# Linear attention feeding an expert router: scores for 64x64 diagonal blocks only, a state in the middle of each chunk, masks on GpSimd

## The chip, the cores and the metric

The kernel runs on one core of a Trainium2 chip. The time is the device time of one execution in microseconds (us), median of three runs; lower is better. A profile is one more execution, recorded by the hardware profiler. The core's engines are TensorE (PE: matmuls and transposes; its weight loads are listed as PEld), VectorE (DVE), ScalarE (ACT), GpSimd (POOL) and SyncE (SP, which here issues most DMAs). Each engine works through its own queue in order, and engines wait for each other on semaphores. Matmul results go to PSUM, of which this kernel uses eight banks; its other tiles are in SBUF.

## What is computed

Gated linear attention with a decay for each channel, then a mixture of experts in which each token goes to one expert. All arrays are float32; B, H, S, D = 4, 8, 768, 48; the 8 x 48 = 384 channels of a token are its row for the router; 8 experts, hidden width 1024.

```python
for t in range(S):
    state = alpha[:, :, t, :, None] * state + np.einsum('bhd,bhe->bhde', k[:, :, t], v[:, :, t])
    y[:, :, t] = np.einsum('bhd,bhde->bhe', q[:, :, t], state)
x = y.transpose(0, 2, 1, 3).reshape(B * S, H * D)
logits = normalized(x) @ normalized(expert_emb).T / tau
e = argmax(logits); g = softmax(logits)[e]
out = g * (relu(x @ w1[e]) @ w2[e])
```

## The kernel before, in words

**Chunks and steps.** The 3072 tokens are 24 chunks of 128 (`NS` = 24; six chunks, `NCH`, to a batch row). Channels lie on partitions after a transpose: a pair of heads, each padded from 48 to 64 channels, fills 128 partitions, so a chunk is a tile of 128 x 512 (4 head pairs x 128 tokens). The main loop (L716) runs `s` = 0 to 26, and a step `s` holds stages of several chunks: chunk `s` is decayed, chunk `s-1` gets its scores, chunk `s-2` its output in columns (channels on partitions), chunk `s-3` its output in rows. "Chunk 20's scores" below are thus made in step 21.

**One chunk, stage by stage.** `load` (L450 to L455) fetches alpha in two pieces, k and q of chunk `s` and v of chunk `s-1` through SP's queue, two steps ahead. `decays` transposes alpha (`pa`) and k (`pk`) on TensorE; VectorE scans alpha backwards (`r`, L477) and multiplies k by it (`kr`, L484); q is transposed too (`pq`). `queries` copies q out of PSUM on ScalarE (`qc`, L493). `decay_queries` scans alpha forwards on VectorE (`a`, L506) and multiplies q by it on GpSimd (`qs`, L510). `scores` multiplies `kr` and `qs` for the whole 128 x 128 block of each head, in 16 matmuls of 64 x 64 x 128 columns; the even heads are masked to the causal half by VectorE (L577, times `causal`), the odd heads copied by ScalarE (L578) and masked by GpSimd (`affine_select`, L579). `keys_back` transposes `kr` back (`pkb`; copied by ScalarE to `kb`, L527); `update` multiplies `kb` and v into `pd`, to which VectorE adds the decayed old state (L560); GpSimd decays the state (`dec`, L535). `mix_states` multiplies the old state with the queries, `mix_chunk` v with the scores, into one PSUM bank for the even and one for the odd heads; ScalarE copies both to `ycols` (L621). `rows` turns them into rows and makes the logits in the same matmuls (16 of 64 x 64 x 56 columns); ScalarE copies rows and logits out (L649, L652), VectorE adds the logits (L653).

**Routing.** Every few chunks (`GROUPS`) `choose` picks each token's expert on VectorE and counts tokens into `before` (mostly on GpSimd, L340; for chunks 15 and 23 on VectorE). `place`, two or four steps later, works out each token's row with a few matmuls, and `to_rows` scatters one chunk of 128 tokens (L311, an indirect DMA issued by GpSimd, one or two in a step, queued behind `qs` of the step). After chunk 15 the first expert is chosen (`first_expert`) and `fetch_early` (L181) loads 256 of its tokens; on SP this stands ahead of `weights(0)` (L141, L144), the 3 MB of that expert's weights.

**The tail.** In steps 24 to 26 the last chunks are finished while TensorE does the first layer for the early tokens (`first_layer_early`, `phe`, 8 products), then the last chunks are scattered, and the experts follow, one after another, from about 158 us to the end.

**Order.** PE's order is written out by hand: `in_turn` queues each group of matmuls behind the one before. `issue_after` does so for other engines. Orders left open are settled by the compiler's scheduler. PSUM: three banks rotate for the transposes (`ps_tr`), two hold scores, two `pyx` (also rows of one half and the ranks of `place`), one the state update and the other half of the rows.

Of the kernel before, what the change touches and what calls it, by code (L numbers as in the profile page):

```python
# [9 lines left out]
FP32 = mybir.dt.float32  # L10
# [17 lines left out]
def kernel(  # L28
# [50 lines left out]
    causal = consts.tile([P, 1, P], FP32)  # L79
# [120 lines left out]
    with ExitStack() as c1:  # L200
        keep = c1.enter_context(tc.tile_pool(name="keep", bufs=1))
        work = c1.enter_context(tc.tile_pool(name="work", bufs=2))
        ps_tr = c1.enter_context(tc.tile_pool(name="ps_tr", bufs=3, space=PSUM))
# [15 lines left out]
        inr = keep.tile([P, NP * P], FP32, name="inr")  # L219

        def fixed_parts():
# [14 lines left out]
            make_upper_triangular(nc, causal[:, 0], val=1.0, diag=True)  # L236
# [35 lines left out]
        def prepare_first(a0):  # L272

            p0 = ps_tr.tile([P, NP, NS], FP32, tag="tr", name="p0")
            for p in range(NP):
                tr(
                    p0[:, p], a0[:, 2 * p : 2 * p + 2].rearrange("s h d -> s (h d)"),
                    ident[:NS, :NS],
                )
            nc.vector.tensor_copy(al0, p0)  # L280
# [18 lines left out]
        def turn_logits():  # L299

            pe = ps_tr.tile([P, 2, NP // 2, E], FP32, tag="tr", name="pe")
# [40 lines left out]
        def place(g, total=False):  # L342
# [4 lines left out]
            bank = y_bank(1)[:, 0 : (GMAX + 1) * E].rearrange("p (s e) -> p s e", e=E)  # L347
# [82 lines left out]
        def turned(t, name):  # L430
            pt = ps_tr.tile([P, NP * P], FP32, tag="tr", name=name)
# [32 lines left out]
        def decays(s):  # L464
# [10 lines left out]
            pa = turned(at_s[i], "pa")  # L475
# [5 lines left out]
            pk = turned(kt_s[i], "pk")  # L481
# [3 lines left out]
            d["pq"] = turned(qt_s[i], "pq")  # L485
            d["a"] = pa, r

        def queries(s, copied):

            d = st[s]  # L490
            d["qc"] = qc = work.tile([P, NP * P], FP32, name="qc")
            with tc.issue_after(copied.ins) if copied else ExitStack():
                nc.scalar.copy(qc, d["pq"])  # L493

        def decay_queries(s):
# [13 lines left out]
            d["qs"] = qs = work.tile([P, NP, P], FP32, name="qs", bufs=4)  # L509
            by_pool = nc.gpsimd.tensor_tensor(  # L510
                qs.rearrange("p n t -> p (n t)"), d["qc"], a, ALU.mult
            )
# [3 lines left out]
            d["last"] = by_dve, by_pool  # L516

        def keys_back(s, ps=ps_tr, tag="tr"):

            if s % NCH == NCH - 1 or "kb" in st[s]:  # L520
                return
            kr = st[s]["kr"]
            pkb = ps.tile([P, NP * P], FP32, tag=tag, name="pkb")
# [5 lines left out]
        def decay_state(s):  # L529

            if s % NCH == 0:
                return
            d = st[s]
            dec = d["dec"] = work.tile([P, NP, DP], FP32, name="dec", bufs=3)
            nc.gpsimd.tensor_tensor(  # L535
                dec, carried["state"], d["end"].to_broadcast([P, NP, DP]), ALU.mult
            )

        def update(s):

            c = s % NCH
            if c == NCH - 1:
                return
            d = st[s]
            kb, vt = d["kb"], vt_s[s % NBV]
            pd = ps_mm.tile([P, NP, DP], FP32, tag="mm", name="pd")
            for p in range(NP):
                for hh in range(2):
                    h = 2 * p + hh
                    mm(  # L550
                        pd[DP * hh : DP * hh + DP, p],
                        lhsT=kb[:, h * DP : (h + 1) * DP],
                        rhs=vt[:, h],
                        start=True, stop=True,
                    )
            carried["state"] = state = work.tile([P, NP, DP], FP32, name="state")
            if c == 0:
                nc.vector.tensor_copy(state, pd)
            else:
                nc.vector.tensor_tensor(state, pd, d["dec"], ALU.add)  # L560

        def scores(s):
# [3 lines left out]
            d["sm"] = sm = [work.tile([P, NP, P], FP32, name=f"sm{hh}") for hh in range(2)]  # L566
            sc = [ps_sc.tile([P, NP, P], FP32, name=f"sc{hh}") for hh in range(2)]
            for p in range(NP):
                for i in range(2):
                    to = slice(i * HALF, (i + 1) * HALF)  # L570
                    for hh in range(2):
                        sl = slice(DP * hh, DP * hh + DP)
                        mm(
                            sc[hh][to, p], lhsT=kr[sl, p, to], rhs=qs[sl, p],
                            start=True, stop=True, skip_group_check=True,
                        )
            nc.vector.tensor_tensor(sm[0], sc[0], causal.to_broadcast([P, NP, P]), ALU.mult)  # L577
            nc.scalar.copy(sm[1], sc[1])  # L578
            d["masked"] = nc.gpsimd.affine_select(  # L579
                out=sm[1], in_=sm[1], pattern=[[0, NP], [1, P]], base=0,  # L580
                channel_multiplier=-1, compare_op=ALU.is_ge, fill=0.0,
            )


# [3 lines left out]

        def y_bank(hh):
            return ps_y.tile([P, 512], FP32, name=f"pyx{hh}")  # L590

        def mix_states(s):
            d = st[s]
            d["pyx"] = pyx = [y_bank(hh) for hh in range(2)]
            dec = d.get("dec")
            if dec is not None:
                for q in range(NQ):
                    for j in range(2):
                        for i in range(2):
                            hh, p = i, 2 * q + (i + j) % 2  # L600
                            sl, to = slice(DP * hh, DP * hh + DP), DP * (p % 2)
                            mm(
                                pyx[hh][to : to + DP, q * P : (q + 1) * P],
                                lhsT=dec[sl, p], rhs=d["qs"][sl, p],
                                start=(q == 0), stop=False, skip_group_check=True,
                            )

        def mix_chunk(s):

            d = st[s]  # L610
            pyx, sm, vt = d["pyx"], d["sm"], vt_s[s % NBV]
            d["yT"] = yT = [work.tile([P, NQ, P], FP32, name=f"ycols{hh}") for hh in range(2)]
            for hh in range(2):
                for p in range(NP):
# [770 lines left out]
```

## Time and profile before

| | |
|---|---|
| median of 3 runs | 412.09 us (411.66 to 412.46) |
| the profiled execution | 410.29 us, of which 408.4 us are the span from its first to its last instruction |
| granted TensorE clock, mean | 0.998 |
| PE busy | 394.4 us (97%) |
| DVE busy | 287.2 us (70%) |
| POOL busy | 221.2 us (54%) |
| ACT busy | 195.9 us (48%) |
| attention steps: first and last group of scores | 12.6 and 139.6 us |

The busy times are over both parts of the program, attention (to about 158 us) and experts. A busy PE need not be one at its peak, as matmuls are pipelined. Times inside the profile are counted from the start of the span. In the lists below, `64*64 64x128` after a matmul means that 64 x 64 of the array is used, with 128 columns streamed; a float32 matmul appears as two instructions, a transpose as one.

### The profile page before, as it was taken

How to read it: one execution, taken by the hardware profiler on the slowest of the kernel's cores; microseconds unless marked ns; L12 is line 12 of the kernel's file. 1: busy time of each engine (PE TensorE's matmuls, PEld its weight loads, DVE VectorE, ACT ScalarE, POOL GpSimd, SP SyncE). 2: the span in 40 equal slices, each digit the busy share in tenths (PEclk: the TensorE clock that was granted, in tenths of full speed). 3: DMA queues.
4: the chain of work that ended last, by engine and by line, in shares of the span. 5: the costliest groups of instructions: out<-in, count | busy, mean ns of one | idle time of the engine just before them, and what ended most of it. 6: DMA issues, size and time to landing. Idle time of an engine off the chain costs nothing. (4 is left out here: it accounts for less than half of the span.)

```text
span 408.4 us, 12552 instructions
## 1 busy us (share of the span) xinstructions
PE 394.4 (97%) x4954; PEld 352.6 (86%) x4954; DVE 287.2 (70%) x634; ACT 195.9 (48%) x481; POOL 221.2 (54%) x288
## 2 busy tenths in 40 slices
PE   7999999999979989999999999999999999999994
PEld 6889989889879777779989889899979979979974
DVE  6899989799799517863695695792694388497530
ACT  3455554555535534564743734824551662662320
POOL 7365687777665447712844835812851582581001
PEclk9999999999999999999999999999999999999999
DMA  9999999999998893786405607406502900001001
GB/s 138 160 161 157 157 189 178 186 188 190 203 184 155 313 377 113 208 324 243 162 18 200 220 19 242 171 19 209 206 19 60 351 3 33 27 2 49 8 17 44
DMA packets 119379, 60.28 MB, mean 148 GB/s; under 512 B 102287, under 2 KB 113816, under 8 KB 119312
## 3 DMA queue, kind: packets, MB, share of 16 engines
q1 hardware_dynamic: 115208, 49.14, 50.1%
q0 software_dynamic: 3728, 10.16, 6.9%
q8 instruction: 46, 0.75, 0.8%
q14 instruction: 21, 0.17, 0.1%
q10 hardware_dynamic: 376, 0.05, 0.1%
HBM read 49.69 MB, written 11.45 MB: 150 GB/s over the span
## 5 line engine op out<-in xcount | busy, mean ns | idle before, releaser
L852 POOL DMA_INDIRECT out_dram<-y,sx x25 | 24.5, 981 | 101.2 <-DVE y L1161 42.3
L982 DVE TENSOR_TENSOR hT<-pq,hT 128x512 f32<-128x512 f32 x63 | 43.6, 692 | 46.1 <-PE pq L1082 44.3
L1082 PE MATMUL pq<-xT_m,w_m 128*128 128x128 f32 x560 | 67.2, 276 | 0.0
L1082 PEld LDWEIGHTS pq<-xT_m,w_m 128*128 128x128 f32 x560 | 64.8, 192 | 0.3 <-issue 0.3
L510 POOL TENSOR_TENSOR qs<-qc,a 128x512 f32<-128x512 f32 x24 | 30.6, 1275 | 33.2 <-DVE a L506 24.1
L1034 POOL TENSOR_TENSOR w_m<-w_m,w 128x512 f32<-128x512 f32 x30 | 43.2, 1446 | 1.4
L965 PE MATMUL pyo<-w,hT 128*128 128x384 f32 x128 | 42.6, 487 | 0.0
L1082 PE MATMUL pq<-xT_m,w 128*128 128x128 f32 x280 | 38.4, 277 | 0.6
L987 ACT ACTIVATE hT<-hT 128x512 f32<-128x512 f32 x35 | 22.1, 631 | 31.3 <-DVE hT L982 31.3
L1082 PEld LDWEIGHTS pq<-xT_m,w 128*128 128x128 f32 x280 | 34.9, 192 | 2.1 <-issue 1.8
L965 PEld LDWEIGHTS pyo<-w,hT 128*128 128x128 f32 x128 | 23.8, 191 | 14.8
L477 DVE TENSOR_TENSOR_SCAN r<-pa,inr 128x511 f32<-128x511 f32 x24 | 29.2, 1216 | 6.3 <-PE pa L194 6.1
L311 POOL DMA_INDIRECT xs<-x,dest x24 | 24.2, 1009 | 11.1 <-DVE x L653 6.2
L506 DVE TENSOR_TENSOR_SCAN a<-pa,ini 128x512 f32<-128x512 f32 x24 | 29.3, 1223 | 1.0
L1154 PE MATMUL pq<-w_m,hT_m 128*128 128x192 f32 x168 | 28.4, 326 | 0.0
L191 PE MATMUL sc<-qs,kr 64*64 64x128 f32 x768 | 27.5, 277 | 0.5 <-issue 0.5
L1154 PEld LDWEIGHTS pq<-w_m,hT_m 128*128 128x128 f32 x168 | 27.5, 190 | 0.0
L191 PE MATMUL pyx<-sm,vt 128*64 128x128 f32 x384 | 26.7, 280 | 0.1
L191 PEld LDWEIGHTS pyx<-sm,vt 128*64 128x64 f32 x384 | 20.4, 136 | 4.7 <-issue 3.4
L1034 POOL TENSOR_TENSOR w_m<-w 128x512 f32<-128x512 f32 x12 | 15.3, 1275 | 15.9 <-PE pq L1082 15.9
L191 PEld LDWEIGHTS sc<-qs,kr 64*64 64x64 f32 x768 | 22.3, 137 | 1.2 <-issue 0.9
L649 ACT COPY lg<-pyx 128x32 f32<-128x32 f32 x24 | 4.4, 185 | 38.8 <-PE px L191 38.8
(229 smaller groups left out, 916.5 us busy)
## 6 DMA issues: line engine op xcount, KB each, us to landing
w<-in_moe_w_dram SPq DMA_DIRECT2D x16, 1536.0 KB, 7.9
kt<-in_k_dram SPq DMA_DIRECT2D x24, 192.0 KB, 4.0
qt<-in_q_dram SPq DMA_DIRECT2D x24, 192.0 KB, 4.9
vt<-in_v_dram SPq DMA_DIRECT2D x24, 192.0 KB, 5.3
xg<-xs SPq DMA_DIRECT2D x22, 196.5 KB, 7.8
at<-in_alpha_dram SPq DMA_DIRECT2D x24, 168.0 KB, 4.8
xg<-xs SPq DMA_DIRECT2D x8, 98.2 KB
at<-in_alpha_dram SPq DMA_DIRECT2D x24, 22.5 KB, 4.4
```

The source lines that it names most:

```text
L191: last["pe"] = nc.tensor.matmul(*args, **kwargs)
L311: ins = nc.gpsimd.indirect_dma_start(out=xs, out_offset=bass.IndirectOffsetOnAxis(ap=rows, axis=0), in_=x, in_offset=None, bounds_check=E ...
L477: nc.vector.tensor_tensor_scan(r[:, L - 2 :: -1], pa[:, L - 1 : 0 : -1], inr[:, L - 2 :: -1], 1.0, ALU.mult, ALU.add,)
L506: d["a_scan"] = by_dve = nc.vector.tensor_tensor_scan(a, pa, ini, 0.0, ALU.mult, ALU.add)
L510: by_pool = nc.gpsimd.tensor_tensor(qs.rearrange("p n t -> p (n t)"), d["qc"], a, ALU.mult)
L852: ins = nc.gpsimd.indirect_dma_start(out=out, out_offset=bass.IndirectOffsetOnAxis(ap=col, axis=0), in_=y, in_offset=None, bounds_check=N - 1,
L965: pe[:] = [nc.tensor.matmul(py, lhsT=hT[:, f], rhs=w2_t[:, f], start=(f == 0), stop=(f == FT - 1),)]
L982: dve[:] = [call(*args, **kwargs)]
L987: act[:] = [call(*args, **kwargs)]
L1034: by(to, x, y, op)
L1082: pe[:] = [nc.tensor.matmul(to[:, f], lhsT=left[:, f * P : (f + 1) * P], rhs=right, start=start and f == 0, stop=stop, skip_group_check=Tr ...
L1154: pe[:] = [nc.tensor.matmul(to, lhsT=left[:, f], rhs=right[:, f], start=start and f == 0, stop=stop and f == n - 1, skip_group_check=True,)]
```

## The change

It changes the attention steps only.

- `scores`: only the two 64 x 64 blocks on the diagonal of each head's 128 x 128 block are made (64 columns rather than 128). ScalarE copies both halves of the heads out of PSUM; GpSimd masks all heads in two passes (partitions 0 to 63, then 0 to 127). The `causal` tile and VectorE's masking are gone.
- `update`: the state is advanced in two halves of 64 tokens, into two PSUM banks. VectorE makes `mid`, the state in the middle of the chunk, and from it the state at its end; both without the padding (192 elements rather than 256). It now also runs for the last chunk of a batch row, for `mid` alone, and so does `keys_back`.
- `mix_states`: the first 64 queries of a chunk use the old state, the later 64 `mid`. `mix_chunk` makes the products of scores and v for the two diagonal blocks, in two passes (`turn` 0 and 1) that alternate the banks.
- Order within a step: the states and pass 0 of chunk `s-2` stand before `rows(s-3)`, the transpose of q after it; `update(s-1)` comes before `scores(s-1)`, pass 1 last. `qs` of step `s` is queued on GpSimd behind the masks of chunk `s-1`.
- PSUM: the three transpose banks have fixed users (`tr0`: q and `pkb`; `tr1`: alpha; `tr2`: k and the first half of the update); `rows` uses the two score banks; `place` uses the `mm` bank.
- The tail's `first_layer_early` is split otherwise: products 0 and 1 in step 24, 2 to 5 in step 25, 6 and 7 in step 26.
- The clearing of `xg` moves from GpSimd (memset) to ScalarE (copies of `blank`).

```diff
-        ps_tr = c1.enter_context(tc.tile_pool(name="ps_tr", bufs=3, space=PSUM))
+        ps_tr = c1.enter_context(tc.tile_pool(name="ps_tr", bufs=1, space=PSUM))
...
+        NST = 3
+        dec_s, mid_s = (
+            [keep.tile([P, NP, DP], FP32, name=f"{name}{i}") for i in range(NST)]
+            for name in ("dec", "mid")
+        )
...
-            bank = y_bank(1)[:, 0 : (GMAX + 1) * E].rearrange("p (s e) -> p s e", e=E)
+            bank = ps_mm.tile([P, 512], FP32, tag="mm", name="ranks")
+            bank = bank[:, 0 : (GMAX + 1) * E].rearrange("p (s e) -> p s e", e=E)
...
-            d["pq"] = turned(qt_s[i], "pq")
...
         def queries(s, copied):
 
             d = st[s]
+            pq = turned(qt_s[s % NBUF], "pq", 0)
...
+        def scaled_queries(s):
+
+            d = st[s]
+            d["qs"] = qs = work.tile([P, NP, P], FP32, name="qs", bufs=4)
+            with ExitStack() as queue:
+                for call in st[s - 1].get("masked", ()) if s else ():
+                    queue.enter_context(tc.issue_after(call.ins))
+                by_pool = nc.gpsimd.tensor_tensor(
+                    qs.rearrange("p n t -> p (n t)"), d["qc"], d["scan"], ALU.mult
+                )
+            d["last"] = *d["last"], by_pool
...
         def update(s):
...
+            halves = [ps_tr.tile([P, NP, D], FP32, tag="tr2", name="pd0")]
+            if c < NCH - 1:
+                halves.append(ps_mm.tile([P, NP, D], FP32, tag="mm", name="pd1"))
             for p in range(NP):
                 for hh in range(2):
                     h = 2 * p + hh
-                    mm(
-                        pd[DP * hh : DP * hh + DP, p],
-                        lhsT=kb[:, h * DP : (h + 1) * DP],
-                        rhs=vt[:, h],
-                        start=True, stop=True,
-                    )
...
+                    for i, pd in enumerate(halves):
+                        mm(
+                            pd[part_of(hh), p],
+                            lhsT=kb[part_of(i), h * DP : (h + 1) * DP],
+                            rhs=vt[part_of(i), h, 0:D],
+                            start=True, stop=True, skip_group_check=True,
+                        )
+            d["mid"] = mid = mid_s[s % NST]
             if c == 0:
-                nc.vector.tensor_copy(state, pd)
+                nc.vector.tensor_copy(mid[:, :, 0:D], halves[0])
             else:
-                nc.vector.tensor_tensor(state, pd, d["dec"], ALU.add)
+                nc.vector.tensor_tensor(
+                    mid[:, :, 0:D], halves[0], d["dec"][:, :, 0:D], ALU.add
+                )
+            if c < NCH - 1:
+                carried["state"] = state = work.tile([P, NP, D], FP32, name="state")
+                nc.vector.tensor_tensor(state, halves[1], mid[:, :, 0:D], ALU.add)
...
                     for hh in range(2):
-                        sl = slice(DP * hh, DP * hh + DP)
                         mm(
-                            sc[hh][to, p], lhsT=kr[sl, p, to], rhs=qs[sl, p],
+                            sc[hh][part_of(i), p], lhsT=kr[part_of(hh), p, part_of(i)],
+                            rhs=qs[part_of(hh), p, part_of(i)],
                             start=True, stop=True, skip_group_check=True,
                         )
-            nc.vector.tensor_tensor(sm[0], sc[0], causal.to_broadcast([P, NP, P]), ALU.mult)
-            nc.scalar.copy(sm[1], sc[1])
-            d["masked"] = nc.gpsimd.affine_select(
...
+            d["sm"] = sm = work.tile([P, 2, NP, HALF], FP32, name="sm")
+            for hh in range(2):
+                nc.scalar.copy(sm[:, hh], sc[hh])
+            d["masked"] = masked = []
+            for i in range(2):
+                x = sm[0 : (i + 1) * HALF].rearrange("s a p t -> s (a p) t")
+                with tc.issue_after(masked[0].ins) if masked else ExitStack():
+                    masked.append(nc.gpsimd.affine_select(
+                        out=x, in_=x, pattern=[[0, 2 * NP], [1, HALF]], base=i * HALF,
+                        channel_multiplier=-1, compare_op=ALU.is_ge, fill=0.0,
+                    ))
...
+            for half in range(2):
+                held = d["mid"] if half else d.get("dec")
...
+                                d["pyx"][hh][part_of(j), c0 : c0 + HALF],
+                                lhsT=held[part_of(hh), p],
+                                rhs=d["qs"][part_of(hh), p, part_of(half)],
+                                start=into(d, hh, j), stop=False, skip_group_check=True,
...
+        def mix_begin(s):
+
+            with in_turn():
+                mix_states(s)
+            with in_turn():
+                mix_chunk(s, 0)
...
+            if 0 < s - 2 < NS:
+                mix_begin(s - 2)
             if 3 <= s <= NS:
                 with in_turn():
                     copied = rows(s - 3)
...
+            if s < NS:
+                scaled(s)
+            if 0 <= s - 1 < NS:
 
                 with in_turn(), tc.issue_after(st[s]["a_scan"].ins) if s < NS else ExitStack():
+                    update(s - 1)
+            if 0 <= s - 1 < NS:
+                with in_turn():
                     scores(s - 1)
+            if s < NS:
+                scaled_queries(s)
...
-                    first_layer_early(2 * (s - NS), 2 * (s - NS) + 1)
+                    first_layer_early(2 * (s - NS), 3 * (s - NS) + 2)
             if 0 <= s - 2 < NS:
                 with in_turn():
-                    mix_states(s - 2)
-                with in_turn():
-                    mix_chunk(s - 2)
...
+                    mix_chunk(s - 2, 1)
...
-                with behind(s):
-                    nc.gpsimd.memset(xg_s[i][:, t], 0.0)
+                with tc.issue_after(st[s - 2]["y_read"].ins):
+                    nc.scalar.copy(xg_s[i][:, t], blank)
```

## The prediction

> **What bounds the kernel now.** I began with the time windows, because the attention steps and the experts behind them are two programs with different limits, and the change touches the first alone. Columns: stretch and length; busy us (instructions) of PE, PEld, DVE, ACT, POOL; granted clock, DMA engines' share, GB/s.
>
> ```profile
> 20.00:40.00 20.00, 19.84 (x478) 18.00 (x476) 18.58 (x35) 10.18 (x33) 12.32 (x25) 1.00 1.02 158
> 60.00:80.00 20.00, 19.95 (x470) 18.14 (x463) 17.58 (x33) 11.36 (x35) 15.24 (x27) 1.00 0.97 188
> 80.00:100.00 20.00, 19.44 (x466) 17.70 (x466) 18.88 (x37) 10.70 (x34) 14.93 (x28) 1.00 0.95 181
> ```
>
> Three things look full: TensorE, VectorE (88 to 94%) and the DMA engines. The timeline of one step (14 to 15) tells what TensorE does; columns are start, length, engine, line, what.
>
> ```profile
> 87.12 1.05 PE L191 MATMUL sc<-qs,kr 64*64 64x128 f32 x30
> 88.55 1.09 PE L191 MATMUL pyx<-sm,vt 128*64 128x128 f32 x16
> 89.47 0.63 PE L191 MATMUL pd<-vt,kb 128*64 128x64 f32 x16
> 90.03 0.66 PE L194 MATMUL pkb<-ident,kr 128*128 128x128 f32 x4
> 90.53 0.60 PE L194 MATMUL pa<-ident,at 128*128 128x128 f32 x4
> ```
>
> From start to start the scores take 0.97 us (from 87.03), the old state's product 0.55, scores times v 0.92, the update 0.56, four groups of transposes 0.44 to 0.50 each, the rows 0.50: 5.3 us without a gap. But SP's timeline says that the loads need as much:
>
> ```profile
> 75.78 1.89 SPq L450 DMA_DIRECT2D at<-in_alpha_dram  x2
> 77.76 1.34 SPq L451 DMA_DIRECT2D kt<-in_k_dram  x1
> 79.19 1.09 SPq L452 DMA_DIRECT2D qt<-in_q_dram  x1
> 80.37 1.43 SPq L455 DMA_DIRECT2D vt<-in_v_dram  x1
> 81.90 2.70 SPq L450 DMA_DIRECT2D at<-in_alpha_dram  x2
> ```
>
> Each issue starts 0.05 us after the last one ended, though the buffers of step 15 were last read in step 11: the queue is pushed against full DMA engines, not held by compute. The same list has alpha of chunk 2 at 7.50 and of chunk 23 at 119.85: 112.35 / 21 = **5.35 us a step**. q of the last chunk is issued at 121.75, lands at about 126.65 (median 4.9) and is transposed at 132.30. So however fast the steps get, they can win 5.65 us on the loads by then, no more. Steps 14 to 18 already ran at 5.3 us (scores at 87.03 and 108.29); most of the lag arises in steps 18 to 22 (scores at 108.29 and 133.61, 6.3 us each), where VectorE waits for GpSimd's count and then works without a gap:
>
> ```profile
> 110.05 0.17 DVE L340 TENSOR_TENSOR before<-before,chosen 128x8 f32<-128x8 f32 x1 [2.02 <-POOL before L340]
> ```
>
> Last, what do the experts wait for? In GpSimd's and SP's timelines the scatter of chunk 15 stands behind `qs` of step 21; the early tokens' load (L181) waits for it (3.7 us in SP's waits), and `weights(0)` stands behind that:
>
> ```profile
> 125.52 1.28 POOL L510 TENSOR_TENSOR qs<-qc,a 128x512 f32<-128x512 f32 x1 [2.00 <-DVE a L506]
> 126.95 1.01 POOL L311 DMA_INDIRECT xs<-x,dest  x1
> ```
>
> ```profile
> 130.02 0.40 SPq L181 DMA_DIRECT2D xg<-xs  x1
> 130.93 0.54 SPq L141 DMA_DIRECT2D w<-in_moe_w_dram  x1
> ```
>
> ```profile
> 139.88 1.56 PE L191 MATMUL phe<-exT,w 128*128 128x256 f32 x6
> ```
>
> A weight load lands 6.8 to 8.7 us after issue (median 7.9), so at about 139: TensorE's first expert product starts right then. **This chain, scatter 15 + 12.9 us = first `phe`, and not TensorE, hands over to the tail.** The page's chain of waits ends in output scatters and says nothing here.
>
> **The change, part by part.** *TensorE.* A group of 32 instructions of 64 x 64 x 56 (rows) takes 0.50 us, of 128 columns 0.97. For 64 columns I take 0.53, nearest the 56-column row; bounds 0.49 (half of 0.97) and 0.97. Scores 0.97 to 0.53; scores times v 0.92 to 0.53; states 0.55 to 0.53; the update, 32 at 48 columns, 0.56 to 0.45 (48/56 of 0.50 is 0.43; bounds 0.36, by the 128-column row, and 0.50). Sum -0.96 us a step; the last chunk of each row gains a `pkb` group and half an update (+0.7, four times). One more switch between 128- and 64-wide products a step: after `pq` the next group starts 0.55 after, between transposes 0.44, so +0.1. TensorE falls to some 4.5 us, below the loads: worth nothing until something else lets it.
>
> The Trainium skill ("TensorEngine Tiling (Array Packing)", Instruction Overhead) speaks against the small columns: a matmul has some 60 cycles of overhead and one column costs as much as 60. By it the 48-column update takes as long as one of 60, an estimated 0.53 us, +0.08 a step, in an engine that has 0.8 to spare. No row before has fewer than 56 columns on four tiles.
>
> *VectorE.* Gone: the mask (L577, 0.68, 0.60 from start to start). The state's add over 256 elements (0.415) becomes two over 192; nearest rows 256 elements 0.415 and a 192-element one with a scalar, 0.413 (L1161); I take 0.35 each, 0.28 from start to start. Net -0.35 a step (bounds -0.1 and -0.4).
>
> *ScalarE.* One copy of 512 (0.63) becomes two of 256 (`ycols`: 0.37 each), +0.11, +0.59 for `kb` in four steps, and twelve clearing copies at 0.48 (L987, 128x384). It is busy 11 of 20 us, 3.0 a step, and gets to 3.7: hidden behind the loads' 5.35; without that cover it would cost 0.1 to 0.7 a step. A mask's copies can be late behind `qc` (0.63) at most.
>
> *GpSimd.* The mask doubles, +0.64 (0.32 if 64 partitions were cheaper); clearing -0.43 in twelve steps; `dec` 0.61 to 0.46. It did 15 of 20 us: total 4.6 us a step with one scatter (masks 1.28, `qs` 1.28, scatter 1.2, the rest 0.9), below 5.35, and 5.9 in the four steps with two.
>
> *What is queued behind what.* `qs` of step s now stands behind the masks of chunk s-1, and those behind its scores, which stand behind `update(s-1)`, which shares bank `tr2` with `pk(s)` and so waits for `kr(s)`. Counted from the start of the backward scan r(s): `kr` done 2.0, update 0.5, scores 0.5, latency 0.3, two copies 0.75, latency 0.1, masks 1.25 (0.6 + 0.64), `qs` 1.27, issue 0.15: the scatter starts **6.8 us after r(s)**, not 126.95 - 122.03 = 4.92. With the loads pacing there is room: scores 0.5, latency and copies 1.05, masks 1.35, then pass 0 of the next step 0.3, the rows 0.5, latency 0.25, their copies 0.8 (they empty the score banks), and scores again: a loop of 4.75 us against 5.35.
>
> **The sum**, on the profiled execution. To step 18 the loads pace; v of chunk 17 is issued at 96.37 and lands (median 5.3) at 101.7, but step 16 (two scatters, a choice: VectorE 4.1 + 1.95) leaves GpSimd late, so the scores of chunk 17 are at about 102.7 (before 103.4 by their successor's pace). Then copies and masks to 105.6, `qs` 106.9, two scatters 109.35, count, and r(19) at 109.75 (before 110.13, -0.4). To r(20) TensorE's round over `kr`, update, scores, `pkb`, `pa` takes 4.4 (before 4.36); to r(21) VectorE is solid, 7.54 - 0.37 = 7.17. r(21) = 121.3 (before 122.03, -0.7). Scatter 15 = 121.3 + 6.85 = 128.15 (**+1.2**); through the unchanged loads the first `phe` is at 141.1 (+1.2). In the tail the scatter of chunks 16 to 19 comes 6.58 us after `phe` before (146.46); after: two `phe` 2.84, pass 1 0.25, wait for `ycols` 0.65, rows 0.65, ranks 0.45, VectorE and GpSimd 0.9 = 5.75 (**-0.85**). From there GpSimd's eight scatters and two pads, 15.4 us to the experts' fetch, stay; the experts are unchanged. Net **+0.35 us**: span 408.75, run 410.6; the profiled run lies 1.8 below the median of 412.09, so **412.4 us**. Its own range, from the bounds (64-column groups ±, mask 0.32, scatter 15 between 127.2 and 129.4): 411.3 to 413.9.
>
> A difference under 0.2% (0.82 us) can't be told from none.
>
> **Rivals.** *A, faster:* masks 20 are done before the forward scan of step 21 (scores 20 don't wait for `kr`, or GpSimd reaches them early). Then scatter 15 is at 121.3 + 4.92 = 126.2 (-0.75) and the net -1.6: 410.5; if r(19) too is up to 1.2 earlier, 409.3. For it: VectorE loses work in all those steps; the loads allow it. Against: the order above, each link in the code. *B, slower:* GpSimd becomes the bound. It can't start masks before ScalarE's copies, so its 4.6 us a step gets idle time between. From 0.75 idle a step it passes 5.35; at 1.1 idle the pitch is 5.7, and (5.7 - 5.35) x 11 scatter steps = 3.9 us: 416. For it: GpSimd's present waits before `qs` (24.1 us in 16 steps for the scan). Against: work can be queued into the gap (`dec`, `end`, counts). *C:* the 64-column products don't shrink and TensorE stays at 5.6: (5.6 - 5.35) x 20 = 5 us, 417; against it the 56-column row.
>
> **Chances.** Forecast 0.50 (faster 0.08, same 0.24, slower 0.18), A 0.21, B 0.26, C 0.03. Together faster 0.29, same 0.24, slower 0.47. Range 408.9 to 416.4: A's lower half and C are mostly outside.
>
> **What would show it.** 32 `sc` instructions in about 0.53 us; SP's loads still 5.35 a step; scatter 15 near 128 and `weights(0)` near 132, against A's 126 and 130; GpSimd's idle time before the masks under 0.75 us a step, against B; TensorE with gaps in the steps. The prediction is wrong if `weights(0)` is put ahead of the early tokens' load, since then the tail is free to start some 1.5 us earlier.

## The result, and the profile after

| | before | after |
|---|---|---|
| median of 4 runs | 412.27 us (411.66 to 417.82) | **435.77 us** (435.48 to 436.51) |
| profiled execution, span | 408.4 us | 433.9 us |
| scatter of chunk 15 | 127.0 | 144.6 (+17.6) |
| first expert product (`phe`) | 139.9 | 162.7 (+22.9) |
| first `pxg` of the experts' fetch | 164.5 | 186.4 (+21.9) |

The changed kernel is slower: ratio 1.0541, 95% interval 1.0450 to 1.0632. The forecast was 412.4 us, with a range of 408.9 to 416.4. Some executions of a kernel show a lower granted clock and are some per cent longer; where two times of one kernel below differ by over 1.5%, the shorter one is compared. Nearly all of the 25.5 us of span are lost before the first expert product. From there to `pxg` it takes 1.0 us less than before; the experts and the last scatters take 3.6 us more (not followed up).

The time windows of the attention steps, after (stretch and length; busy us and instructions of PE, PEld, DVE, ACT, POOL; granted clock, DMA engines' share, GB/s):

```profile
20.00:40.00 20.00, 16.42 (x564) 14.20 (x563) 16.03 (x34) 9.81 (x32) 10.99 (x24) 1.00 0.95 156
60.00:80.00 20.00, 16.49 (x538) 14.48 (x536) 13.71 (x27) 10.91 (x36) 15.42 (x26) 1.00 0.97 186
80.00:100.00 20.00, 15.81 (x530) 13.63 (x529) 13.61 (x29) 10.13 (x34) 12.52 (x20) 1.00 0.99 180
```

TensorE was busy 19.4 to 19.95 of 20 us before and is now busy 15.8 to 16.5, VectorE 13.6 to 16.0 instead of 17.6 to 18.9. No engine is full; only the DMA engines still are. Yet a step got longer: from chunk 4's scores to chunk 21's it was 5.55 us a step and is 6.19. This measure is used for every run below.

TensorE's waits up to the first expert product (tile, what it waited for, total us, times, longest):

```profile
PE sc L190 <- issue: 9.4, 8, 2.5
PE pyx L190 <- POOL sm L614: 7.9, 8, 1.7
PE pyx L190 <- issue: 4.8, 5, 1.1
PE pkb L193 <- issue: 3.3, 2, 2.8
PE pd L190 <- issue: 2.0, 2, 1.4
```

Before, the same list came to 4.5 us, with these two lines for the longest wait and for "issue":

```profile
PE px L191 <- DVE state L560: 2.1, 3, 1.4
PE sc L191 <- issue: 0.5, 1, 0.5
```

Now it is 30.7: 7.9 for GpSimd's masks, and 19.9 put down to "issue", time in which TensorE waited for nothing that the profile shows. Such a gap, in the timeline of TensorE (start, length, engine, line, operation, in brackets the idle time before):

```profile
68.88 0.68 PE L190 MATMUL pd<-vt,kb 64*64 64x48 f32 x32
69.38 0.65 PE L190 MATMUL sc<-qs,kr 64*64 64x64 f32 x28
71.19 0.27 PE L190 MATMUL sc<-qs,kr 64*64 64x64 f32 x2 [1.16 <-issue]
71.20 0.27 PE L190 MATMUL pyx<-sm,vt 64*64 64x64 f32 x2
```

It falls between two products of one group, whose operands are there. What is it? The list of DMA queues has one that the prediction did not read. First TensorE's busy time and instruction count and that queue (packets, MB, share) before, then the same of after:

```profile
PE 394.4 (97%) x4954; PEld 352.6 (86%) x4954; DVE 287.2 (70%) x634; ACT 195.9 (48%) x481; POOL 221.2 (54%) x288
...
q8 instruction: 46, 0.75, 0.8%
```

```profile
PE 389.8 (90%) x6122; PEld 345.7 (80%) x6122; DVE 274.1 (63%) x640; ACT 201.0 (46%) x521; POOL 230.0 (53%) x298
...
q8 instruction: 55, 0.90, 0.9%
```

Matmuls and weight loads together are 2336 more, and 2336 / 9 = 260: a packet of 16 KB for about every 256 TensorE instructions. A step had 256 of them and now has 352. I numbered TensorE's instructions in order of time. The 18 "issue" gaps before the first expert product, 19.9 us in all, lie at numbers 1218, 1475, 1730, 1986, 2242, 2754 and so on to 8130 (waits on semaphores and branches counted too), all multiples of 256 apart within one. Beside them the packets of q8 (an ordinary list, from the trace's records; a block is the 256 instructions between two such numbers):

```
kernel   block begun   next packet starts   ends     next block begun   gap
before    81.47         +1.63               +2.68     +6.11              -
before    98.44         +2.25               +3.45     +5.14              -
after     67.21         +1.62               +2.57     +3.98             1.16
after     71.19         +3.00               +4.46     +5.83             1.45
after     86.18         +1.70               +3.16     +4.77             1.94
after    149.95         +3.47               +4.40     +5.83             2.75
after    155.78         +4.06               +5.09     +6.65             2.46
```

When a block is begun, the packet for the one behind it starts 1.8 us later (mean from 30 to 135 us), takes 1.2, and after a gap TensorE goes on 1.24 to 1.76 us (mean 1.5) after the packet's end. Together 4.5 us on average, which the block being worked off must last; single packets start 0.8 to 3.0 us after the block. Before, the shortest block between 30 and 140 us lasted 4.93 us; the changed kernel, whose step of 352 holds 4.8 us of work (shown below), would be through 256 in 3.5.

### The profile page after: what moved, and what is told of

Same layout as the page of the kernel before. It is cut to its first block, busy times and chain, and to the rows that moved or that the text cites. A ratio compares the mean times of both kernels' runs of the same rounds, so it can differ in the third digit from the quotient of the medians.

```text
span 433.9 us, 14963 instructions
## 1 busy us (share of the span) xinstructions
PE 389.8 (90%) x6122; PEld 345.7 (80%) x6122; DVE 274.1 (63%) x640; ACT 201.0 (46%) x521; POOL 230.0 (53%) x298
## 5 line engine op out<-in xcount | busy, mean ns | idle before, releaser
L911 POOL DMA_INDIRECT out_dram<-y,sx x25 | 24.6, 983 | 102.1 <-DVE y L1220 42.3
L614 POOL TENSOR_SCALAR_AFFINE_SELECT sm<-sm 64x512 f32<-64x512 f32 (+1 forms) x48 | 31.4, 655 | 15.5 <-ACT sm L609 13.8
L1024 PEld LDWEIGHTS pyo<-w,hT 128*128 128x128 f32 x128 | 23.7, 190 | 14.8
L190 PE MATMUL pyx<-sm,vt 64*64 64x64 f32 x768 | 22.9, 224 | 11.0 <-POOL sm L614 7.9
L709 ACT COPY lg<-sc 128x32 f32<-128x32 f32 x48 | 9.3, 194 | 43.8 <-PE sc L190 43.8
L190 PEld LDWEIGHTS pyx<-sm,vt 64*64 64x64 f32 x768 | 17.4, 134 | 13.5 <-POOL sm L614 9.2
L609 ACT COPY sm<-sc 128x256 f32<-128x256 f32 x48 | 15.5, 375 | 26.4 <-PE sc L190 25.6
L190 PE MATMUL sc<-qs,kr 64*64 64x64 f32 x768 | 19.1, 222 | 8.7 <-issue 8.3
```

The costliest lines, as they stand in the source:

```text
L190: last["pe"] = nc.tensor.matmul(*args, **kwargs)
L614: masked.append(nc.gpsimd.affine_select(out=x, in_=x, pattern=[[0, 2 * NP], [1, HALF]], base=i * HALF, channel_multiplier=-1, compare_op=A ...
L911: ins = nc.gpsimd.indirect_dma_start(out=out, out_offset=bass.IndirectOffsetOnAxis(ap=col, axis=0), in_=y, in_offset=None, bounds_check=N - 1,
L1024: pe[:] = [nc.tensor.matmul(py, lhsT=hT[:, f], rhs=w2_t[:, f], start=(f == 0), stop=(f == FT - 1),)]
```

## The experiments

**Theories.** *Fetch*: more TensorE instructions, fetched in blocks through DMA engines that the loads fill, stop TensorE at block ends. *Loop* (in the prediction 4.75 us around): scores, copies, GpSimd's masks, pass 0 and rows wait for each other. In two of the six sessions the kernel before took 417.5 and 417.7 us, in the others 410.3 to 412.3; the kernels profiled there show gaps of TensorE of some 0.3 us about every 11 us, most of them not at block ends. So runs are compared within a session, and those two are named "the slower chips".

**1. Instructions alone, no change of order** (`more_products`):

```diff
-   mm(sc[hh][to, p], lhsT=kr[sl, p, to], rhs=qs[sl, p], ...)
+   for c in (slice(0, HALF), slice(HALF, P)):
+       mm(sc[hh][to, p, c], lhsT=kr[sl, p, to], rhs=qs[sl, p, c], ...)
...
-   mm(pyx[hh][to : to + DP, q * P : (q + 1) * P], lhsT=dec[sl, p], rhs=d["qs"][sl, p], ...)
+   for c in (0, HALF):
+       mm(pyx[hh][to : to + DP, q * P + c : q * P + c + HALF],
+          lhsT=dec[sl, p], rhs=d["qs"][sl, p, c : c + HALF], ...)
```

> The kernel before, with the scores and the old state's product made in pieces of 64 columns instead of 128: the same work in the same order, but 352 instead of 256 TensorE instructions a step (matmuls and weight loads), as many as the changed kernel has. Theory Fetch (TensorE's instructions arrive in blocks of 256, and with the loads filling the DMA engines a block takes 4.5 to 4.8 us to come, so a step of 352 can't be shorter than some 6.2 us): step 5.9 to 6.3 us, gaps of TensorE that nothing in the program explains at every 256th instruction, 425 to 436 us. Theory Loop (the changed order, in which scores, copies, masks on GpSimd, pass 0 and rows wait for each other, takes 6.2 us around): this order isn't touched, so the step stays at 5.3 to 5.5 us and the time at 412 to 416 us.

Measured: 431.4 and 438.7 us, where before took 410.7. The profile is of the 438.7 us, at a granted clock of 0.979, so its step of 6.52 us is a little too long (5.9 to 6.3 expected). TensorE's waits there, and one gap:

```profile
PE sc L191 <- issue: 6.3, 6, 2.8
PE pd L191 <- issue: 5.8, 5, 2.3
PE pyx L191 <- issue: 2.4, 2, 1.5
PE px L191 <- DVE state L560: 1.2, 2, 0.8
```

```profile
129.01 0.39 PE L191 MATMUL pd<-vt,kb 128*64 128x64 f32 x6
131.66 0.80 PE L191 MATMUL pd<-vt,kb 128*64 128x64 f32 x10 [2.26 <-issue]
```

The kernel before, with nothing changed but the number of products, loses 20.8 us, and its 14 "issue" gaps (14.9 us up to the first expert product) lie at block ends. Loop is not needed for gaps like these. But they are not the whole loss: from chunk 4 to chunk 21 the step grew by 0.97 us, of which the gaps are 0.56. The rest is no gap at a block end: part may be the low clock, part the time that the added instructions take in TensorE itself, since here, unlike in the changed kernel, no columns are saved. So that 20.8 us come near the changed kernel's loss is partly chance.

**2. The loads taken away.** The edit: alpha, k and q are loaded for `s < 4` only. First the changed kernel, then `more_products`, then the kernel before:

> The changed kernel without the loads of alpha, k and q from chunk 4 on (those chunks compute on what lies in the buffers; v is still loaded), so that three quarters of the loads' packets are gone from the DMA engines. Theory Fetch: a block of instructions comes faster, the gaps at block ends vanish or shrink under 0.3 us, the step falls to 4.8 to 5.4 us, and the first expert product starts 15 to 25 us earlier. Theory Loop: none of the waits goes through a load, so the step stays at 6.0 to 6.3 us and the gain is under 4 us.

> The kernel before with the scores and the old state's product in 64-column pieces (352 TensorE instructions a step; the step was 6.1 us), now without the loads of alpha, k and q from chunk 4 on. Theory Fetch (blocks of 256 instructions are slow to come only while the loads fill the DMA engines): the gaps at block ends vanish, the step is back at 5.0 to 5.4 us, the first expert product starts at 135 to 143 us. Rival (so many small products are slow in the array itself, whatever the DMA engines do): the step stays at 5.8 to 6.2 us.

> The kernel before without the loads of alpha, k and q from chunk 4 on. The prediction's reading was that the loads pace its steps at 5.35 us with TensorE's 5.3 just behind; then steps 6 to 18 take 5.2 to 5.3 us and the time falls by at most 1 to 3 us, by what fuller DMA engines add here and there. If the loads held more than that (TensorE's transposes waiting for data, scatters slowed), it falls by 4 us or more. If instruction blocks were late here too, gaps of TensorE outside its waits vanish; the trace of before has one of 0.45 us, so this is worth under 0.5 us.

| kernel, without those loads | time | before, same session | step | gaps at block ends |
|---|---|---|---|---|
| changed | 422.8 | 410.7 | 5.80 (was 6.19) | 2, 0.5 us in all (was 18) |
| `more_products` (slower chip) | 432.2 | 417.7 | 5.93 (was 6.52) | 2 in the steps, 0.4 us in all, and one of 3.87 |
| before (slower chip) | 416.3, ratio 0.9959 (0.9916 to 1.0001) | 417.7 | 5.72 | none |

A window of the changed kernel without the loads, and its waits up to 150 us:

```profile
60.00:80.00 20.00, 17.88 (x612) 16.11 (x616) 14.82 (x32) 12.30 (x41) 15.45 (x26) 1.00 0.29 75
```

```profile
PE pyx L190 <- POOL sm L614: 14.3, 14, 2.9
```

With the DMA share at 0.29 the packets start 1.0 us after a block is begun, not 1.8, and TensorE works through 612 matmuls in 20 us where it had 538. The gaps are gone and the first product comes at 149.1, 13.6 us earlier (15 to 25 expected). But the step misses its 4.8 to 5.4 us: the waits for the masks grew from 7.9 to 14.3. Here Loop is right, behind Fetch. `more_products` missed its 5.0 to 5.4 too: 5.93 lies in the range that its rival gave, small products that are slow in the array itself. It fell on a slower chip; against the kernel before without loads, in the same session, its step is 0.21 us longer, and so much the small products seem to cost by themselves. Its time stays 15.9 us longer than that kernel's: 3.5 between chunks 4 and 21, 3.9 in the gap, which starts at 142 us under the bulk load of the first expert's weights (not taken away), and the rest later, mostly in the tail, where one run doesn't tell the cause. And the kernel before gains at most 0.84% without the loads: they were not alone in pacing it.

**3. The masks.** GpSimd's two `affine_select` over 8 columns in place of 512, first with the loads, then without (twice, since the first fell on a slower chip, with a control beside the second):

> The changed kernel with GpSimd's two masks made over 8 columns instead of 512 (so the scores stay unmasked), which takes some 1.1 of their 1.4 us out of the way from the scores to pass 0 and to the next queries. Theory Fetch: the masks weren't what TensorE waited for at most steps, so the step stays within 0.2 us of 6.2 and the time at 430 to 436 us. Theory Loop: the loop is 1.1 us shorter, the step falls to 5.1 to 5.4 us, and the time to 412 to 420 us.

> The changed kernel with both taken away: no loads of alpha, k and q from chunk 4 on, and GpSimd's masks over 8 columns only, the scores unmasked (without those loads alone the step was 5.7 us, with thin masks alone 6.2). If two limits lie behind each other, the fetch of instructions at 6.2 us and the loop through the masks at 5.7: TensorE's 11.5 us of waits for the masks vanish and the step is 5.0 to 5.3 us. If the 5.7 us are something else (VectorE, the array itself): 5.6 to 5.8 us.

> The changed kernel without the loads of alpha, k and q from chunk 4 on, once more, as the measure for the next run on the same chip: 5.7 to 5.9 us a step, with TensorE's waits for GpSimd's masks 10 to 13 us in all.

> The same with GpSimd's masks over 8 columns only (scores unmasked), once more, since the first one fell on a chip on which the kernel before takes 417.7 us. If the loop through the masks is the limit behind the fetch: 0.4 to 0.7 us a step less than the run before it in this list. If not: within 0.2 us of it.

With the loads: a step of 5.99 us, first product at 157.0 (162.7 with the masks), 436.4 and 438.8 us (ratio 1.0660, 1.0589 to 1.0730; unmasked scores also send the tokens to other experts, so its total is no measure of the masks). Without the loads: 5.92 on the slower chip, nothing to be told from it; then, side by side, 5.88 with the masks and **5.30** without, and the first product at 152.9 and 138.8. The 5.88 were measured at a mean clock of 0.971; the first run without loads, on the same chip at 0.991, had 5.80. The waits of the last one up to 140 us:

```profile
PE pyx L190 <- POOL sm L615: 2.7, 5, 0.9
PE pyx L190 <- issue: 2.1, 2, 1.4
```

So masks are worth 0.2 us a step while the fetch is slow and 0.50 to 0.58 once it is not: two limits, one behind the other. Only with both gone does the changed kernel's step fall below the 5.55 us that the kernel before has with all its loads and masks.

**4. Fewer instructions in the changed kernel**: `rows` in 8 products of 64 x 128 x 56.

```diff
-   for i in range(2):
-       to = slice(i * HALF, (i + 1) * HALF)
-       for j in range(2):
-           mm(px[j][to, hh, q], lhsT=yT[hh][sl, q, to], rhs=sel[sl, hh, q], ...)
+   for j in range(2):
+       mm(px[j][:, hh, q], lhsT=yT[hh][sl, q], rhs=sel[sl, hh, q], ...)
```

> The changed kernel with the rows made in 8 products of 64 x 128 x 56 instead of 16 of 64 x 64 x 56: 320 instead of 352 TensorE instructions a step, about the same time in the array, the same order and the same waits. Theory Fetch: the step falls in proportion, 6.2 x 320/352 = 5.65 us, and the time by 23 x 0.55 = 13 us, to 420 to 427 us. Theory Loop: the rows take no less time, so 433 to 437 us.

Measured: 431.9 and 438.5 us; span 429.9, step 6.06, first product 158.7. That is between the two ranges: too little for Fetch, too much for Loop. The group of the rows here, and the same group in the changed kernel (shapes, count, busy us, mean ns, idle before), both from 30 to 150 us:

```profile
L190 PE MATMUL sc<-sel,ycols 64*128 64x56 f32 x320 | 22.5, 278 | 0.5 <-issue 0.5
```

```profile
L190 PE MATMUL sc<-sel,ycols 64*64 64x56 f32 x608 | 13.2, 218 | 1.1 <-issue 1.1
```

"About the same time in the array" was wrong: in the timeline 16 instructions of 64 x 128 take 1.03 us from start to start, 32 of 64 x 64 take 0.57. The gaps at block ends did fall, from 19.9 to 5.1 us in all; of the 14.8 us, 23 x 0.46 = 10.6 went back into the rows, and the first product came 4.0 us earlier. The run doesn't settle the size by itself, but its parts agree with Fetch.

**5. Dose.** All four block products in halves (416 instructions a step), and only the old state's (288):

> The kernel before with all four of its block products in halves of their columns (scores, old state, scores times v, update): 416 TensorE instructions a step instead of 256, order and work as before. Theory Fetch: the step goes with the count, 416/256 x (4.5 to 4.8) = 7.3 to 7.8 us, where 352 gave 6.1 to 6.5; the time 455 to 475 us. Rival (the 352 were slow for another reason, such as the extra weight loads of two products): half as much again as from 256 to 352, so 6.6 to 7.0 us a step and 438 to 448 us.

> The kernel before with only the old state's product in halves of its columns: 288 TensorE instructions a step instead of 256. Theory Fetch: in the trace of before a block's packet starts 1.7 us after the block ahead of it is begun, takes 1.2 us, and (in the changed kernel) TensorE goes on 1.4 us after its end, so 4.3 us a block, 288/256 x 4.3 = 4.8 us a step, still under the 5.3 us that the work takes: within 3 us of before, one to four short gaps. Rival (each added pair of product and weight load costs its share, 96 of them 22 us): 7 us, so 417 to 420 us.

416: 443.8 us (ratio 1.0786, 1.0720 to 1.0852), a step of 6.96, gaps at 15 block ends. That is in the rival's ranges of time and of step, and short of mine. Of the 1.41 us that the step grew, gaps at block ends are 0.71 (12.0 us between chunks 4 and 21); the other half is no gap, so it seems that the split products cost about as much again by themselves. 288, on a slower chip: 423.0 against 417.5 (1.0130, 1.0061 to 1.0199), two gaps at block ends, 0.28 and 1.13 us. The interval, 2.5 to 8.3 us, holds my 3 us and the rival's 7, so the time decides nothing. And the fetch is no fixed rate of 4.5 to 4.8 us a block: with 416 the blocks between 30 and 140 us last 4.42 us on average and 3.68 at the least, with the changed kernel's 352 4.55 and 3.64. Time is lost at each block whose own 256 instructions are done before the next packet is usable, and that depends on what lies in it: dense 64-column groups run out, transposes last. What remains open is how much of 288's 5.5 us is fetch; the gaps at block ends are 1.4 of them.

**6. The last steps.** The two longest gaps, 2.75 and 2.46 us, come when `weights(0)` runs (issued at 149.9). First the load was only queued in another place, where it started at 150.85 all the same; then a write into its buffer behind the last masks held it back:

> The changed kernel with the load of the first expert's weights put behind the last masks of the attention steps, so that no bulk load runs while TensorE does the last steps. Theory Fetch: the two gaps of 2.75 and 2.46 us at block ends (153.0 and 160.0 us) shrink to under 0.6 us, and the last scores come at 153.5 to 156 us instead of 159.1; the first expert product then waits for its weights, some 8 us after the masks, and the time is no better. Rival (those gaps have to do with something else in the last steps): they stay, the last scores at 158 to 160 us.

> The changed kernel with the load of the first expert's weights held back until GpSimd has done the last masks of the attention steps (a write into the weights' buffer behind them). Theory Fetch: the gaps of 2.75 and 2.46 us at block ends (at 153 and 160 us in the changed kernel) shrink to under 0.6 us each, and the last scores come 3 to 5 us earlier against the ones before them (in the changed kernel 7.3 us after chunk 22's; then 4 to 5). The first expert product waits for its weights, so the time is no better. Rival (something else in the last steps): the gaps stay, and chunk 23's scores come 7 us or more after chunk 22's.

The first try (446.7 us, on a slower chip) moved nothing and tells nothing: gaps of 2.86 and 0.89. In the second (443.3 us), SyncE's queue, and TensorE's waits from 135 to 170 us:

```profile
149.61 0.40 SPq L180 DMA_DIRECT2D xg<-xs  x1
161.55 0.38 SPq L140 DMA_DIRECT2D w<-in_moe_w_dram  x1
```

```profile
PE phe L190 <- DMA w<-in_moe_w_dram: 8.9, 1, 8.9
PE pyx L190 <- POOL sm L614: 2.3, 2, 1.7
```

No gap at a block end is left after 133.6 us, and chunk 23's scores come 5.2 us after chunk 22's (7.4 before the edit; 4 to 5 expected). The bulk load made those gaps. As forecast, the time is then lost waiting for the weights.

**7. Parts of the change without TensorE instructions.** Masking by GpSimd for the even heads too, in the kernel before; the other split of the early products with the clearing by ScalarE (`before_tail`, twice); the split alone; and both with the state in 48 columns (`before_tail_narrow`).

> The kernel before with one part of the change alone: the even heads' scores too are copied by ScalarE and masked by GpSimd, not by VectorE; full 128 x 128 blocks, TensorE's instructions and order as before. Theory Loop (the way through copies and two GpSimd masks, 1.4 us, is too long for the order): TensorE waits for the second mask 0.3 to 0.6 us a step, 415 to 424 us. Theory Fetch alone: no more instructions than before and less for VectorE, so 408 to 412 us.

> The kernel before with the two parts of the change that add no TensorE instruction in the steps: the other split of the first layer's early products in the tail, and the clearing of xg by ScalarE. The prediction's price for the tail was 0.85 us gained, for the clearing 0.43 us less GpSimd in twelve steps, mostly hidden: 1.0 to 0.3 us faster than before. Rival: the products put together let TensorE's rows wait for ScalarE, and ScalarE's twelve copies come in the way of the steps' copies: 0 to 2 us slower.

> The kernel before with the other split of the early products and the clearing by ScalarE, once more. If the 1.4 us gained belong to the kernel: 0.2 to 0.6% faster than before again. If they belong to the chip of the first run: between the same and 1% slower, as the split alone was on the other chip.

> The kernel before with the other split of the early products alone (without the clearing by ScalarE). The prediction gave the tail of the change 0.85 us: 0.5 to 1.0 us faster than before if the gain of both parts together (1.4 us) is the split's; within 0.3 us of before if it was the clearing.

> The kernel before with all parts of the change that add no TensorE instruction: the split of the early products, the clearing by ScalarE, and the state without its padding (48 instead of 64 columns in the update, 192 instead of 256 elements in the decayed state and its sum). TensorE has 0.1 us a step less, GpSimd 0.15, VectorE 0.07. If TensorE's work paces the steps: 1.4 us as before_tail and 1 to 2 us more, 407.5 to 408.5 us where before takes 411. If the loads pace them: as before_tail, within 0.4 us.

| kernel | time | before, same session | ratio (95%) | step |
|---|---|---|---|---|
| `before_pool_masks` (slower chip) | 420.8 | 417.7 | 1.0070 (1.0026 to 1.0115) | 5.67 |
| `before_tail` | 409.5 | 410.9 | 0.9958 (0.9933 to 0.9984) | 5.51 |
| `before_tail_b` | 409.7 | 410.3 | 0.9982 (0.9951 to 1.0012) | 5.51 |
| `before_split` (slower chip) | 422.1 | 417.5 | 1.0090 (1.0057 to 1.0123) | 5.74 |
| `before_tail_narrow` (slower chip) | 421.3 | 417.5 | 1.0071 (1.0037 to 1.0104) | 5.68 |

In the old order GpSimd's second mask makes TensorE wait nowhere; the step of 5.67 us is no longer than the 5.72 of the kernel before without loads in the same session, so the loss of 0.7% is probably not in the steps. The tail's parts gain 1.4 us on one chip, 0.6 (within the noise) on another, and kernels with them lose on a third. No version here can be called better than the kernel before.

## Why the prediction was wrong

**Failed: the price of TensorE's work.** "TensorE falls to some 4.5 us, below the loads" counted the array's time alone. The sizes of the groups were nearly right: 32 `sc` instructions take 0.48 us (forecast 0.53), the 48-column update 0.50 (forecast 0.45); without a wait the work is 4.8 us a step (in the changed kernel without loads, from `pq` at 76.56 to `pq` at 81.36). The Trainium skill's rule ("TensorEngine Tiling (Array Packing)", Instruction Overhead), by which 48 columns cost as much as 60, was nearer than my 48/56. But three of the groups were written down with 32 instructions where there had been 16 (scores times v, the states, the update), and the count that comes of it, 256 to 352 a step with the weight loads, was never priced. From it come 19.9 of the 26.2 us by which TensorE's waits up to the first product grew; experiments 1, 2 and 6 show the cause. The first expert product is 22.9 us later, so the array's smaller work, the pipeline's emptying at each gap included, gave back only 3.3.

A page could have warned: the Trainium skill's "Runtime: NRT & Kernel Launch" (Instruction fetch mechanics) has instructions refilled in blocks of 16 KiB, 256 instructions, over the sequencer's own DMA queue. The packets here agree. It also says that a block boundary's cost is "mostly hidden"; with loads at a DMA share of 0.97 it is not, at 0.9 us a gap on average over the 16 gaps in the steps, and up to 2.75 us under a bulk load.

**Failed: the loop of 4.75 us.** Without the fetch in the way the step is 5.80 to 5.88 us and the masks are worth 0.50 to 0.58 of it. The loop's own terms were nearly right: from chunk 11's scores at 83.69 to chunk 12's at 88.60 the changed kernel takes 4.91 us. What it left out is GpSimd's other work in front of the masks, `dec`, which waits for VectorE's `state`, and the counts. The prediction had `dec` in GpSimd's sum, but put both at nothing in the loop; elsewhere they spoke against B ("work can be queued into the gap"). Chunk 21 shows it: its scores start at 145.15, ScalarE's copies end at 146.51, and GpSimd then does this:

```profile
146.94 1.04 POOL L346 TENSOR_TENSOR before<-before,chosen 128x8 f32<-128x8 f32 x4 [1.13 <-DVE chosen L343]
147.94 0.51 POOL L555 TENSOR_TENSOR dec<-state,end 128x192 f32<-128x192 f32 x1
148.40 1.38 POOL L614 TENSOR_SCALAR_AFFINE_SELECT sm<-sm 64x512 f32<-64x512 f32 x2
```

TensorE's waits for the masks from 135 to 170 us (the longest is the one before pass 0 of chunk 21, at 149.83):

```profile
PE pyx L190 <- POOL sm L614: 2.9, 3, 1.7
```

In the changed kernel without the loads, among chunks 3 to 21, TensorE waits for the masks of the 11 chunks whose first mask starts 0.5 to 3.5 us after the copies' end, and not for those of the 8 where it starts within 0.4. No run moved `dec` or the counts behind the masks, so what this order is worth is not measured. Rival B had the time's sign and a pitch of 5.7, and GpSimd is at the centre of this second limit. But B's cause, idle time before the masks for ScalarE's copies, is not it: the masks' idle time is 15.5 us over 24 chunks, 0.65 us each, under the 0.75 that B needs.

**Failed: "the loads pace".** SyncE's queue at the end of the loads:

```profile
126.61 0.47 SPq L459 DMA_DIRECT2D qt<-in_q_dram  x1
128.32 7.12 SPq L462 DMA_DIRECT2D vt<-in_v_dram  x2
148.94 0.40 SPq L180 DMA_DIRECT2D xg<-xs  x1
149.86 0.38 SPq L140 DMA_DIRECT2D w<-in_moe_w_dram  x1
```

(The issues in the prediction's lines are 0.09 us apart, not 0.05; nothing rests on it.) q of the last chunk is issued at 126.6 and transposed at 150.7, 24 us later and not 10.6 as before, and the last two loads of v, whose buffers come free with the steps, are spread over 7 us; past the first steps TensorE waits for no load. And the kernel before gains at most 0.84% without them.

**Not in the sum: the run-up.** At chunk 4's scores the changed kernel is already 6.1 us late (39.9 against 33.7). Two block-end gaps, 0.56 us at 34.8 and 1.30 at 39.9, are 1.9 of it. The waits up to 34 us name a bank with fixed users (`p` waits for `qc`), `pkb` waiting for VectorE, and 2.0 us for masks; argued from these, not tried.

**Failed: scatter 15 at 128.15.** The chain was 6.8 us from r(21); measured 8.5. VectorE's scan of chunk 21, GpSimd's `qs` and its scatter:

```profile
136.04 1.22 DVE L484 TENSOR_TENSOR_SCAN r<-pa,inr 128x511 f32<-128x511 f32 x1
```

```profile
143.12 1.28 POOL L535 TENSOR_TENSOR qs<-qc,a 128x512 f32<-128x512 f32 x1
144.56 1.01 POOL L317 DMA_INDIRECT xs<-x,dest  x1 [0.15 <-issue]
```

The links were the right ones, but chunk 20's scores came 4.0 us after the scan's start and not 2.5, behind pass 0, which waited 1.05 us for the masks of chunk 19. The other 14.0 of the +17.6 are the lateness of the scan (136.04 against 122.03), the sum of all steps.

**Failed: "scatter 15 + 12.9 us = first `phe`".** It is 18.2. TensorE at the hand-over:

```profile
159.15 0.82 PE L190 MATMUL sc<-qs,kr 64*64 64x64 f32 x23
162.44 0.38 PE L190 MATMUL sc<-qs,kr 64*64 64x64 f32 x9 [2.46 <-issue]
162.75 2.86 PE L190 MATMUL phe<-exT,w 128*128 128x256 f32 x12
```

The order of the loads is unchanged, as assumed (149.86 in the queue above; the median from issue to landing is 7.9 us, so some 158). But TensorE, held up twice by the bulk load, arrives after the weights and hands over itself.

**Right:** the tail's term, -0.85 us (24.6 to 23.6 from the first product to `pxg`); that 64-column groups shrink, against rival C; TensorE with gaps, though of another kind.

## What to carry to other kernels

Before cutting products into smaller ones, count the instructions, weight loads too: divide the time of a stretch by its blocks of 256 and compare that with what a block needs to arrive under that stretch's DMA load (here 4.5 us; about 6 under a bulk load). An "issue" gap between two products of one group, at a multiple of 256 instructions from the last one, is the sign. When an engine's limit is lifted on paper, look for the limits behind it one by one: here the fetch hid the loop through the masks, and in that loop an engine's other work stood in front of the link that was counted.

## What was not expected of the hardware

- A block's packet starts only 1.0 us after the block ahead is begun with the DMA engines 0.27 to 0.3 busy, 1.8 with them full, 3.4 to 4.8 under the bulk load of weights; its 16 KB take 1.1 to 1.2 us in the first two cases, and TensorE goes on some 1.5 us after its end.
- A 64 x 128 product of 56 columns takes 64 ns (16 in 1.03 us), as against 18 ns for a 64 x 64 one (32 in 0.57): half the instructions, 1.8 times the time.
- The kernel before takes 1.7% longer on two chips (417.6 against 410.7 us) at nearly the same mean clock (0.99). The kernels profiled there show short gaps of TensorE about every 11 us; the cause stays open.
